# Batch 0's queries in one load, and the last 128 tokens stored in output order by one transfer per column piece, in a linear-attention and SwiGLU kernel

## The chip, the cores and the metric

The kernel runs on one core of a Trainium2 chip. The metric is the device time of that core in microseconds (us), as the median of three executions. The profile is of one execution; its span goes from the first to the last instruction and is a little shorter than the device time.

The core has a matmul engine (PE), a vector engine (DVE), an engine for activation functions (ACT), a general engine (POOL) and a sync engine (SP). Data moves between device memory and on-chip memory by DMA, issued here from SP (queue 1, and ACT for two stores at the end) and from POOL (queue 0, which also casts float32 to bfloat16). PE writes to PSUM, which has eight banks here, each [128 partitions x 512] float32.

## The reference

An attention without a softmax over pairs, then a SwiGLU feed-forward block over all tokens:

```python
# q, k, v: [8 batches, 8 heads, 576 positions, 64], float32
q_s = softmax of q over the 64 features
k_s = softmax of k over the 576 positions
kv  = einsum('bhsd,bhse->bhde', k_s, v)        # a 64x64 matrix for each head
att = einsum('bhsd,bhde->bhse', q_s, kv)
x   = att.transpose(0, 2, 1, 3).reshape(4608, 512)
g   = x @ w_gate                               # [512, 1536]
out = ((g * sigmoid(g)) * (x @ w_val)) @ w_out # [1536, 512]
```

The output is [4608, 512] in float32.

## The kernel before

Tokens of a batch are held in an order of their own. Position s of a batch is s = 9 p + t, with p from 0 to 63 and t from 0 to 8; a partition of the loaded tiles holds nine neighbouring positions of one head. The transposed attention output `xt` has column 64 t + p of a batch. The nine t are handled in two groups, `BANKS = ((0, 5), (5, 9))`, of 320 and 256 tokens. Four heads make a group `G` (two groups, `NG`), and batch 0 is computed by code of its own, in which loads and the first matmuls are laid beside each other.

The loads at the start, the first exponentials and the weight loads (cuts are marked with `# ...`):

```python
kd = []
for G in range(NG):
    load("q", q, 0, G, BANKS[:1] if G == 1 else ((0, T),))
    kd.append(load("k", k, 0, G))
d = nc.gpsimd.dma_start(out=v16[0], in_=head_ap(v, 0, 0))
tc.add_manual_dep(d.ins, kd[0].ins.name, SYNC, reason="order of loads")
for t0, t1 in BANKS:
    nc.gpsimd.dma_start(out=v16[1][:, :, 64 * t0:64 * t1], in_=head_ap(v, 0, 1, t0, t1))
# ...
exp_of("q", 0, 0, BANKS)
exp_of("k", 0, 0)
exp_of("q", 0, 1, BANKS[:1])
first = norm_sum(0, 0, BANKS)
norm_mul(0, 0, BANKS)
norm_sum(0, 1, BANKS[:1])

for c0, n in ((0, 128), (128, 128), (256, 128), (384, 256), (640, 384), (1024, 512)):
    w_slice(wg, moe_w_gate, c0, n)
    w_slice(wv, moe_w_val, c0, n)
    if c0 == 0:
        t0, t1 = BANKS[1]
        nc.gpsimd.dma_start(
            out=raw["q", 0, 1][:, :, 64 * t0:64 * t1], in_=head_ap(q, 0, 1, t0, t1)
        )
w_dma = [wo_slice(m0, 3) for m0 in (0, 3, 6, 9)]
```

`spin` runs matmuls on zeros. `key_sum` and `kv_first` are matmuls over the exponentials of the keys, `scale_first` divides and gives `kn`, `turn_pe` transposes the normalised queries on PE into a PSUM bank, `turn_out` copies them out, `x_mm` forms the attention output and `x_out` copies it to `xt`. A bank of PSUM comes free for its next use when its reader is done. The order at the start of the feed-forward part, with blocks 0 and 1 of the 12 blocks of 128 hidden columns in parts by bank (`i`) and by group (`G`):

```python
spin(8)
spin(6, first)
key_sum(0)
turn_pe(0, 0, 0)
turn_pe(0, 0, 1)
turn_out(0, 0, 0, nc.scalar)
exp_of("k", 0, 1)
turn_out(0, 0, 1, nc.scalar)
norm_mul(0, 1, BANKS[:1])
spin(6)
kv_first(0)
key_sum(1)
scale_first(0, nc.scalar)
turn_pe(0, 1, 0)
turn_out(0, 1, 0, nc.vector)
xp0 = x_mm(0, 0, 0), x_mm(0, 0, 1)
kv_first(1, *BANKS[0])
kv_first(1, *BANKS[1])
# ... scale_first(1), the copies x_out of group 0
x_out(0, 1, 0, x_mm(0, 1, 0))
exp_of("q", 0, 1, BANKS[1:])
norm_sum(0, 1, BANKS[1:])
norm_mul(0, 1, BANKS[1:])
# ...
part_mm(0, 0, 0)
part_mm(0, 0, 1)
sg0 = part_silu(0, 0)
part_mm(1, 0, 0)
turn_pe(0, 1, 1)
turn_out(0, 1, 1, nc.vector)
part_mul(0, 0, sg0)
part_mm(1, 0, 1)
sg1 = part_silu(1, 0)
part_mm(0, 1, 0)
x_out(0, 1, 1, x_mm(0, 1, 1))
part_mul(1, 0, sg1)
part_mm(1, 1, 0)
part_mm(0, 1, 1)
# ... silu and product of the second bank, part_mm(1, 1, 1)

after = w_dma[0]          # batch 1's loads wait for the first slice of w_out
# ... loads of batches 1 to 3 on SP
for m in range(2, MT):
    m_unit(0, S, m)
# ... batch 1's exponentials, output matmuls of the first tokens, its transposes,
# its kv matmuls, and then a loop over chunks of 512 tokens
```

A block of the hidden layer (`m_unit`), the stores and the end of the kernel:

```python
def m_unit(c0, n, m, by_group=False):
    ms = slice(m * 128, (m + 1) * 128)
    parts = [(c0, n)] if n <= 512 else [(c0, 320), (c0 + 320, n - 320)]
    # ... gate (g_ps) and value (u_ps): four matmuls each for each part
    for g_ps, u_ps, (c, w_) in zip(gu[0], gu[1], parts):
        r = c % RING
        sg = ff.tile([128, 512], BF16, tag="sg", name="sg")
        nc.scalar.activation(out=sg[:, 0:w_], in_=g_ps[:, 0:w_], func=AF.Silu)
        nc.vector.tensor_mul(hr[:, m, r:r + w_], sg[:, 0:w_], u_ps[:, 0:w_])

    def store(j, o_sb, c0=0, c1=512, engs=(nc.sync, nc.sync)):
        for half in range(2):
            b, t = divmod(2 * j + half, T)
            dst = bass.AP(
                tensor=out.tensor,
                offset=out[b * S + t, c0].offset,
                ap=[[T * d_model, 64], [1, c1 - c0]],
            )
            engs[half].dma_start(out=dst, in_=o_sb[64 * half:64 * half + 64, c0:c1])

    def o_last(j):
        r0 = (j * 128) % RING
        o_sb = osb.tile([128, 512], FP32, tag="o_sb", name="o_sb")
        for c0, n in ((0, 320), (320, 192)):
            o_ps = bank("o_ps")
            for m in range(MT):
                nc.tensor.matmul(
                    out=o_ps[:, 0:n], lhsT=hr[:, m, r0:r0 + 128], rhs=wo[:, m, c0:c0 + n],
                    start=(m == 0), stop=(m == MT - 1),
                )
            nc.vector.tensor_copy(out=o_sb[:, c0:c0 + n], in_=o_ps[:, 0:n])
            store(j, o_sb, c0, c0 + n, (nc.sync, nc.scalar))
# ...
        o_unit(jo + 3)
        last = n_tok // 128 - 4
        for j in range(last, last + 3):
            o_unit(j)
        o_last(last + 3)
```

A block of 128 output tokens holds two values of t, 64 positions each, so it is stored by two transfers, one from partitions 0 to 63 and one from 64 to 127. The rows of one transfer lie nine rows apart in the output.

Of the kernel before, what the change touches and what calls it, by code (L numbers as in the profile page):

```python
# [15 lines left out]
def kernel(  # L16
# [10 lines left out]
    nc = tc.nc  # L27
# [55 lines left out]
    def load_kv(b):  # L83
        whole = ((0, T),)
        last = b == B - 1
        for G in range(NG):
            load("k", k, b, G, BANKS if last else whole)
            load("v", v, b, G, BANKS if last and G == 0 else whole)

# [26 lines left out]
    def exp_of(what, b, G, pieces=((0, T),)):  # L116
        s = st.setdefault((b, G), {})
        if "e" + what not in s:
            s["e" + what] = at.tile([128, T, 2, 64], BF16, tag="e" + what, name="e" + what)
        e = s["e" + what]  # L120
        src = raw[what, b, G].rearrange("p h (t d) -> p t h d", d=64)
        for t0, t1 in pieces:
            nc.scalar.activation(out=e[:, t0:t1], in_=src[:, t0:t1], func=AF.Exp)  # L123
# [7 lines left out]
    def norm_sum(b, G, pieces=((0, T),)):  # L131
        s = st[b, G]
        eq2 = s["eq"].rearrange("p t h d -> p (t h) d")
        if "rs" not in s:
            s["rs"] = at.tile([128, 2 * T], FP32, tag="rs", name="rs")
            s["rr"] = at.tile([128, 2 * T], FP32, tag="rr", name="rr")
        rs, rr = s["rs"], s["rr"]
# [6 lines left out]
        r = slice(2 * pieces[0][0], 2 * pieces[-1][1])  # L144
        nc.vector.reciprocal(out=rr[:, r], in_=rs[:, r])
        return first

    def norm_mul(b, G, pieces=((0, T),), engs=None):
        s = st[b, G]
        eq2 = s["eq"].rearrange("p t h d -> p (t h) d")  # L150
        if "qs" not in s:
            s["qs"] = at.tile([128, T, 128], BF16, tag="qs", name="qs")
        qs = s["qs"]
# [124 lines left out]

    def m_unit(c0, n, m, by_group=False):
        ms = slice(m * 128, (m + 1) * 128)  # L280
# [14 lines left out]
        for g_ps, u_ps, (c, w_) in zip(gu[0], gu[1], parts):  # L295
            r = c % RING
            sg = ff.tile([128, 512], BF16, tag="sg", name="sg")
            nc.scalar.activation(out=sg[:, 0:w_], in_=g_ps[:, 0:w_], func=AF.Silu)  # L298
            nc.vector.tensor_mul(hr[:, m, r:r + w_], sg[:, 0:w_], u_ps[:, 0:w_])  # L299

    def store(j, o_sb, c0=0, c1=512, engs=(nc.sync, nc.sync)):
        for half in range(2):
            b, t = divmod(2 * j + half, T)
            dst = bass.AP(
                tensor=out.tensor,
                offset=out[b * S + t, c0].offset,
                ap=[[T * d_model, 64], [1, c1 - c0]],
            )
            engs[half].dma_start(out=dst, in_=o_sb[64 * half:64 * half + 64, c0:c1])

# [19 lines left out]
    def o_last(j):  # L330
        r0 = (j * 128) % RING
        o_sb = osb.tile([128, 512], FP32, tag="o_sb", name="o_sb")
        for c0, n in ((0, 320), (320, 192)):
            o_ps = bank("o_ps")
# [5 lines left out]
            nc.vector.tensor_copy(out=o_sb[:, c0:c0 + n], in_=o_ps[:, 0:n])  # L340
            store(j, o_sb, c0, c0 + n, (nc.sync, nc.scalar))

# [3 lines left out]
    with tc.manual_schedule():  # L346
        kd = []
        for G in range(NG):
            load("q", q, 0, G, BANKS[:1] if G == 1 else ((0, T),))
            kd.append(load("k", k, 0, G))  # L350
# [30 lines left out]
        w_dma = [wo_slice(m0, 3) for m0 in (0, 3, 6, 9)]  # L381
# [63 lines left out]
        x_out(0, 0, 1, xp0[1])  # L445
        x_out(0, 1, 0, x_mm(0, 1, 0))
        exp_of("q", 0, 1, BANKS[1:])
        norm_sum(0, 1, BANKS[1:])
        norm_mul(0, 1, BANKS[1:])

        parts = [(64 * t0, 64 * (t1 - t0)) for t0, t1 in BANKS]
        gu = {}

        def part_mm(m, i, G):
            c, w_ = parts[i]
            if G == 0:
                gu[m, i] = bank("g_ps"), bank("u_ps")
            for a in range(2):
                for kk in (2 * G, 2 * G + 1):
                    nc.tensor.matmul(  # L460
                        out=gu[m, i][a][:, 0:w_], lhsT=(wg, wv)[a][:, kk, m * 128:(m + 1) * 128],
                        rhs=xt[:, kk, c:c + w_], start=(kk == 0), stop=(kk == KT - 1),
                    )

        def part_silu(m, i):
            w_ = parts[i][1]
            sg = ff.tile([128, 512], BF16, tag="sg", name="sg")
            nc.scalar.activation(out=sg[:, 0:w_], in_=gu[m, i][0][:, 0:w_], func=AF.Silu)
            return sg

        def part_mul(m, i, sg):
            c, w_ = parts[i]
            nc.vector.tensor_mul(hr[:, m, c:c + w_], sg[:, 0:w_], gu[m, i][1][:, 0:w_])

        part_mm(0, 0, 0)
        part_mm(0, 0, 1)
        sg0 = part_silu(0, 0)
        part_mm(1, 0, 0)
        turn_pe(0, 1, 1)
        turn_out(0, 1, 1, nc.vector)  # L480
        part_mul(0, 0, sg0)
        part_mm(1, 0, 1)
        sg1 = part_silu(1, 0)
        part_mm(0, 1, 0)
        x_out(0, 1, 1, x_mm(0, 1, 1))
        part_mul(1, 0, sg1)
        part_mm(1, 1, 0)
        part_mm(0, 1, 1)
        part_mul(0, 1, part_silu(0, 1))
        part_mm(1, 1, 1)  # L490
        part_mul(1, 1, part_silu(1, 1))

# [12 lines left out]

        for m in range(2, MT):
            m_unit(0, S, m)

# [49 lines left out]
        for ci, (c0, n) in enumerate(chunks):  # L558
# [5 lines left out]
            for m in range(MT):  # L564
# [79 lines left out]
```

## Time and profile before

| what | before |
|---|---|
| time, median of 3 | 314.97 us (314.6 to 315.17) |
| span of the profiled execution | 312.8 us |
| mean granted clock of PE | 0.996 |
| busy: PE, weight loads, DVE, ACT, POOL | 303.6, 150.0, 161.4, 146.2, 32.6 us |
| matmuls | 2182 |
| read from and written to device memory | 37.75 and 9.44 MB |
| end of the last PE instruction | about 307.9 us |

Busy time is a sum over the whole span, and PE's is modelled; so it says which engine is full, and the stretches and waits say when it isn't. A row of the profile names engine, source line, operation, output and inputs; behind an arrow in brackets stands what ended the idle time before it. `xN` means that N such instructions are merged in the row.

### The profile page before, as it was taken

The numbers are of one execution on the slowest core, as the hardware profiler recorded it, in microseconds if no ns is written. First come the engines' busy times: TensorE is split into PE (matmuls) and PEld (weight loads), VectorE is DVE, ScalarE is ACT, GpSimd is POOL, SyncE is SP. The second block draws the span as 40 slices with busy tenths as digits, with TensorE's granted clock in tenths as the row PEclk, the third lists the DMA queues.
The fourth block names the chain that finished last, engine by engine and source line by source line (L and its number), as shares of the span: only waits on it lengthen the run. The fifth ranks groups of instructions, "written<-read, shape, count | busy, mean of one in ns | idle before, by whom it ended". The sixth has DMA issues, their size and how long they took to land.

```text
span 312.8 us, 5455 instructions
## 1 busy us (share of the span) xinstructions
PE 303.6 (97%) x2182; PEld 150.0 (48%) x2182; DVE 161.4 (52%) x275; ACT 146.2 (47%) x214; POOL 32.6 (10%) x40
## 2 busy tenths in 40 slices
PE   6989999999999999999999999999999999999993
PEld 2568754555444544454444444544444444444442
DVE  3664477956763567355826492639353324333321
ACT  5653377794764465547364737455043113212200
POOL 2970011420200110002000200000000000000000
PEclk9999999999999999999999999999999999999998
DMA  7999999999355906491629352605310211021033
GB/s 266 183 191 206 264 390 385 353 181 377 107 105 137 385 14 133 91 385 49 143 67 339 119 116 62 185 0 106 72 34 0 69 25 42 3 67 31 2 80 91
DMA packets 42586, 45.78 MB, mean 146 GB/s; under 512 B 19584, under 2 KB 27520, under 8 KB 42560
## 3 DMA queue, kind: packets, MB, share of 16 engines
q1 hardware_dynamic: 33568, 39.72, 43.5%
q0 software_dynamic: 8832, 5.57, 12.1%
q8 instruction: 17, 0.28, 0.4%
q10 hardware_dynamic: 160, 0.13, 0.2%
q14 instruction: 9, 0.07, 0.1%
HBM read 37.75 MB, written 9.44 MB: 151 GB/s over the span
## 4 chain that ended last, share of the span: by engine, by line
PE 93%; DMA 3%; POOL 2%; ACT 0%; issue 0%; SPq 0%; DVE 0%
PE g_ps L291 30%; PE u_ps L291 29%; PE o_ps L316 29%; DMA wv<-in_moe_w_val_dram 2%; DMA k<-in_k_dram 2%; PE kv L196 2%; PE xp L252 1%; PE o_ps L336 1%; PE u_ps L460 1%; POOL wg L96 0%; POOL v L354 0%; PE tp L171 0%; PE g_ps L460 0%; POOL v L351 0%; POOL wv L96 0%; POOL q L378 0%
## 5 line engine op out<-in xcount | busy, mean ns | idle before, releaser
L298 ACT ACTIVATE sg<-g_ps 128x512 bf16<-128x512 f32 (+2 forms) x116 | 63.2, 559 | 132.7 <-PE g_ps L291 132.3
L299 DVE TENSOR_TENSOR hr<-sg,u_ps 128x512 bf16<-128x512 bf16 (+2 forms) x116 | 72.5, 636 | 85.0 <-PE u_ps L291 81.0
L291 PE MATMUL g_ps<-xt,wg 128*128 128x512 bf16 (+2 forms) x464 | 108.9, 360 | 0.1
L291 PE MATMUL u_ps<-xt,wv 128*128 128x512 bf16 (+2 forms) x464 | 108.9, 360 | 0.0
L316 PE MATMUL o_ps<-wo,hr 128*128 128x512 bf16 x420 | 93.9, 379 | 0.0
L291 PEld LDWEIGHTS <-wv 128*128 128x128 bf16 x464 | 45.4, 98 | 46.0
L291 PEld LDWEIGHTS <-wg 128*128 128x128 bf16 x464 | 44.8, 98 | 44.9 <-issue 0.4
L316 PEld LDWEIGHTS <-hr 128*128 128x128 bf16 x420 | 40.9, 98 | 48.6
L110 DVE COPY o_sb<-o_ps 128x512 f32<-128x512 f32 x33 | 22.4, 680 | 39.2 <-PE o_ps L316 39.2
L126 POOL CAST vb<-v 128x1152 bf16<-128x1152 f32 x14 | 16.9, 1211 | 138.7 <-DMA v<-in_v_dram 102.9
L140 DVE TENSOR_REDUCE rs<-eq 128x18 f32<-128x1152 bf16 (+2 forms) x18 | 21.8, 1214 | 13.2 <-ACT eq L123 13.2
L156 DVE TENSOR_TENSOR qs<-eq,rr 128x1152 bf16<-128x1152 bf16 (+2 forms) x18 | 22.1, 1233 | 0.2
L123 ACT ACTIVATE eq<-q 128x1152 bf16<-128x1152 f32 (+2 forms) x18 | 18.3, 1051 | 2.9 <-DMA q<-in_q_dram 2.8
L123 ACT ACTIVATE ek<-k 128x1152 bf16<-128x1152 f32 (+2 forms) x17 | 17.9, 1102 | 0.2
L298 ACT ACT_TABLE_LOAD x11 | 14.1, 1283 | 0.2
L123 ACT ACT_TABLE_LOAD x11 | 14.1, 1283 | 0.2
L386 PE MATMUL idle<-zero 128*128 128x512 bf16 x20 | 7.8, 555 | 2.9 <-DVE rs L140 1.6
L266 ACT CAST xt<-xp 128x512 bf16<-128x512 f32 x14 | 7.8, 586 | 5.2 <-PE xp L252 5.2
L267 DVE CAST xt<-xp 128x512 bf16<-128x512 f32 x14 | 9.0, 683 | 0.7 <-PE xp L252 0.7
L196 PEld LDWEIGHTS <-ek 64*64 64x64 bf16 x504 | 6.3, 107 | 1.7 <-ACT qt L108 0.4
L196 PE MATMUL kv<-vb,ek 64*64 64x65 bf16 x504 | 6.8, 194 | 0.0
L252 PE MATMUL xp<-qt,kn 64*64 64x512 bf16 (+1 forms) x112 | 6.7, 292 | 0.0
(51 smaller groups left out, 80.0 us busy)
## 6 DMA issues: line engine op xcount, KB each, us to landing
out_dram<-o_sb SPq DMA_DIRECT2D x70, 128.0 KB, 2.3
q<-in_q_dram SPq DMA_DIRECT2D x15, 576.0 KB, 5.3
k<-in_k_dram SPq DMA_DIRECT2D x13, 576.0 KB, 7.9
v<-in_v_dram SPq DMA_DIRECT2D x13, 576.0 KB, 8.9
wo<-in_moe_w_out_dram POOLq DMA_DIRECT2D x4, 384.0 KB, 15.2
k<-in_k_dram SPq DMA_DIRECT2D x3, 320.0 KB, 7.7
k<-in_k_dram SPq DMA_DIRECT2D x3, 256.0 KB, 7.9
wg<-in_moe_w_gate_dram POOLq DMA_DIRECT2D x1, 512.0 KB, 10.6
```

The lines of the kernel that those rows point to most:

```text
L110: eng.tensor_copy(out=out, in_=in_)
L123: nc.scalar.activation(out=e[:, t0:t1], in_=src[:, t0:t1], func=AF.Exp)
L126: return nc.gpsimd.tensor_copy(out=vbs[G][:, :, :, 0:64], in_=raw["v", b, G].rearrange("p h (t d) -> p t h d", d=64),)
L140: i = nc.vector.reduce_sum(out=rs[:, 2 * t0:2 * t1], in_=eq2[:, 2 * t0:2 * t1, :], axis=mybir.AxisListType.X)
L156: last = eng.tensor_mul(qs[:, t0:t1, :].rearrange("p t (h d) -> p (t h) d", d=64), eq2[:, 2 * t0:2 * t1, :], s["rr"][:, 2 * t0:2 * t1].to_ ...
L196: nc.tensor.matmul(out=kv[g][HALF[h], c:c + 65], lhsT=ek[HALF[g], t, h, :], rhs=vbs[G][HALF[g], t, h, :], start=(t == 0), stop=(t == T - 1),)
L252: nc.tensor.matmul(out=o[h][HALF[g], c:c + 64 * (t1 - t0)], lhsT=kn[HALF[h], g, G, :], rhs=qt[G][HALF[h], t0:t1, 64 * g:64 * g + 64], star ...
L267: nc.vector.tensor_copy(out=xt[:, 2 * G + 1, c0:c0 + 512], in_=main[G][1])
L291: nc.tensor.matmul(out=gu[a][i][:, 0:w_], lhsT=(wg, wv)[a][:, kk, ms], rhs=xt[:, kk, c:c + w_], start=(kk == 0), stop=(kk == KT - 1),)
L298: nc.scalar.activation(out=sg[:, 0:w_], in_=g_ps[:, 0:w_], func=AF.Silu)
L299: nc.vector.tensor_mul(hr[:, m, r:r + w_], sg[:, 0:w_], u_ps[:, 0:w_])
L316: nc.tensor.matmul(out=o_ps, lhsT=hr[:, m, r0:r0 + 128], rhs=wo[:, m, :], start=(m == 0), stop=(m == MT - 1),)
```

## The change

At the start, batch 0's second query group is loaded whole, ahead of the second keys; the late load on POOL's queue and the staged order of blocks 0 and 1 are gone, and `m_unit` makes all twelve blocks. At the end, the last 128 tokens are put in pair order when the hidden values are written: column 2 p + h takes the place of 64 h + p. Then partitions 2 p and 2 p + 1 of the last output block hold two neighbouring rows of the output, and one transfer over 64 row pairs stores a column piece, in place of two. The 320-column piece goes by ACT, the 192-column piece by SP. Some loads of batches 6 and 7 are also split in two.

```diff
-            load("k", k, b, G, BANKS if last else whole)
-            load("v", v, b, G, BANKS if last and G == 0 else whole)
+            load("k", k, b, G, BANKS if last or (b == B - 2 and G == 1) else whole)
+            load("v", v, b, G, BANKS if last else whole)
 # ... (m_unit)
-            nc.vector.tensor_mul(hr[:, m, r:r + w_], sg[:, 0:w_], u_ps[:, 0:w_])
+            w1 = w_ - 128 if final else w_
+            nc.vector.tensor_mul(hr[:, m, r:r + w1], sg[:, 0:w1], u_ps[:, 0:w1])
+            if final:
+                nc.vector.tensor_mul(
+                    hr[:, m, r + w1:r + w_].rearrange("k (p h) -> k h p", h=2),
+                    sg[:, w1:w_].rearrange("k (h p) -> k h p", h=2),
+                    u_ps[:, w1:w_].rearrange("k (h p) -> k h p", h=2),
+                )
 # ... (o_last)
-        for c0, n in ((0, 320), (320, 192)):
+        b, t = divmod(2 * j, T)
+        for c0, n, eng in ((0, 320, nc.scalar), (320, 192, nc.sync)):
 # ...
-            store(j, o_sb, c0, c0 + n, (nc.sync, nc.scalar))
+            dst = bass.AP(
+                tensor=out.tensor,
+                offset=out[b * S + t, c0].offset,
+                ap=[[T * d_model, 64], [d_model, 2], [1, n]],
+            )
+            eng.dma_start(out=dst, in_=o_sb[:, c0:c0 + n])
 # ... (the start)
-            load("q", q, 0, G, BANKS[:1] if G == 1 else ((0, T),))
+            load("q", q, 0, G)
 # ...
-        exp_of("q", 0, 1, BANKS[:1])
+        exp_of("q", 0, 1, BANKS)
 # ...
-        norm_sum(0, 1, BANKS[:1])
+        norm_sum(0, 1, BANKS)
 # ...
-            if c0 == 0:
-                t0, t1 = BANKS[1]
-                nc.gpsimd.dma_start(
-                    out=raw["q", 0, 1][:, :, 64 * t0:64 * t1], in_=head_ap(q, 0, 1, t0, t1)
-                )
 # ...
-        norm_mul(0, 1, BANKS[:1])
+        norm_mul(0, 1, BANKS)
 # ...
         turn_pe(0, 1, 0)
+        turn_pe(0, 1, 1)
         turn_out(0, 1, 0, nc.vector)
+        turn_out(0, 1, 1, nc.vector)
 # ...
-        x_out(0, 1, 0, x_mm(0, 1, 0))
 # ... (the late exponential, sum and product; part_mm, part_silu, part_mul and their order: removed)
+        xp1 = x_mm(0, 1, 0), x_mm(0, 1, 1)
+        x_out(0, 1, 0, xp1[0])
+        x_out(0, 1, 1, xp1[1])
 # ...
-        for m in range(2, MT):
-            m_unit(0, S, m)
+        for m in range(MT):
+            m_unit(0, S, m, by_group=(m == 0))
 # ...
-                m_unit(c0, n, m, by_group=(ci == 0 and m == 0))
+                m_unit(c0, n, m, by_group=(ci == 0 and m == 0), final=final)
```

More of the change, by code (lines that the diff above doesn't have):

```diff
@@ L117, in exp_of @@
         s = st.setdefault((b, G), {})
-        if "e" + what not in s:
-            s["e" + what] = at.tile([128, T, 2, 64], BF16, tag="e" + what, name="e" + what)
-        e = s["e" + what]
+        e = s["e" + what] = at.tile([128, T, 2, 64], BF16, tag="e" + what, name="e" + what)
         src = raw[what, b, G].rearrange("p h (t d) -> p t h d", d=64)
@@ L133, in norm_sum @@
         eq2 = s["eq"].rearrange("p t h d -> p (t h) d")
[L134 to L137, printed above, removed]
+        rs = at.tile([128, 2 * T], FP32, tag="rs", name="rs")
         first = None
@@ L143, in norm_sum @@
             first = first or i
-        r = slice(2 * pieces[0][0], 2 * pieces[-1][1])
-        nc.vector.reciprocal(out=rr[:, r], in_=rs[:, r])
+        rr = s["rr"] = at.tile([128, 2 * T], FP32, tag="rr", name="rr")
+        nc.vector.reciprocal(out=rr, in_=rs)
         return first
@@ L150, in norm_mul @@
         eq2 = s["eq"].rearrange("p t h d -> p (t h) d")
-        if "qs" not in s:
-            s["qs"] = at.tile([128, T, 128], BF16, tag="qs", name="qs")
-        qs = s["qs"]
+        qs = s["qs"] = at.tile([128, T, 128], BF16, tag="qs", name="qs")
         for (t0, t1), eng in zip(pieces, engs or (nc.vector, nc.vector)):
@@ L275, in x_and_next_kv, with m_unit @@
             scale_both(b + 1)
-    def m_unit(c0, n, m, by_group=False):
+    def m_unit(c0, n, m, by_group=False, final=False):
         ms = slice(m * 128, (m + 1) * 128)
@@ L298, in m_unit, with store @@
             nc.scalar.activation(out=sg[:, 0:w_], in_=g_ps[:, 0:w_], func=AF.Silu)
-            nc.vector.tensor_mul(hr[:, m, r:r + w_], sg[:, 0:w_], u_ps[:, 0:w_])
-    def store(j, o_sb, c0=0, c1=512, engs=(nc.sync, nc.sync)):
+            w1 = w_ - 128 if final else w_
[6 more added lines that the diff above has]
+                )
+    def store(j, o_sb):
         for half in range(2):
@@ L305, in store @@
                 tensor=out.tensor,
-                offset=out[b * S + t, c0].offset,
-                ap=[[T * d_model, 64], [1, c1 - c0]],
+                offset=out[b * S + t, 0].offset,
+                ap=[[T * d_model, 64], [1, d_model]],
             )
-            engs[half].dma_start(out=dst, in_=o_sb[64 * half:64 * half + 64, c0:c1])
+            nc.sync.dma_start(out=dst, in_=o_sb[64 * half:64 * half + 64, :])
     def o_mm(j, o_ps=None, m0=0, m1=MT):
@@ L445 @@
         x_out(0, 0, 1, xp0[1])
-        x_out(0, 1, 0, x_mm(0, 1, 0))
[L447 to L491, printed above, removed]
+        xp1 = x_mm(0, 1, 0), x_mm(0, 1, 1)
+        x_out(0, 1, 0, xp1[0])
+        x_out(0, 1, 1, xp1[1])
         after = w_dma[0]
```

## The prediction

> **What bounds the kernel now.** I read the chain that ended last first, then busy time by stretch, then the two ends in order of time, because a nearly full engine leaves only the ends to gain. Part 4 of the page (shares of the span by engine):
>
> ```profile
> PE 93%; DMA 3%; POOL 2%; ACT 0%; issue 0%; SPq 0%; DVE 0%
> ```
>
> The matmul engine (PE) carries 93%. Busy time by stretch (start:end, length, then PE, weight loads, DVE, ACT, POOL in us with counts, granted clock, DMA share, GB/s):
>
> ```profile
> 20.00:100.00 80.00, 79.92 (x696) 45.34 (x695) 48.53 (x87) 49.47 (x76) 11.49 (x10) 1.00 0.92 248
> 100.00:200.00 100.00, 100.00 (x791) 46.77 (x790) 56.55 (x90) 55.61 (x72) 6.91 (x6) 1.00 0.57 165
> 200.00:295.00 95.00, 95.00 (x454) 43.02 (x455) 41.28 (x64) 29.10 (x47) 0.00 (x0) 1.00 0.18 40
> ```
>
> From 20 us to 295 us PE idles 0.08 us in all, at full clock. The change leaves the useful matmuls as they are in number and width, so the time can move in two places: how early PE becomes full, and how long the end lasts after its last matmul. The start, in order of time (start, duration, engine, line, what, idle before):
>
> ```profile
> 14.09 0.45 PE L460 MATMUL g_ps<-xt,wg 128*128 128x320 bf16 x2
> ...
> 16.34 0.11 PEld L460 LDWEIGHTS <-wg 128*128 128x128 bf16 x2 [1.15 <-DMA wg<-in_moe_w_gate_dram]
> ...
> 16.89 0.11 PEld L460 LDWEIGHTS <-wv 128*128 128x128 bf16 x2 [0.43 <-DMA wv<-in_moe_w_val_dram]
> ...
> 20.15 1.14 PE L291 MATMUL g_ps<-xt,wg 128*128 128x320 bf16 x8
> ```
>
> The first feed-forward matmul starts at 14.09, and the third block (m=2) at 20.15. Between them lie blocks 0 and 1. A block of 576 tokens takes 1.96 us (the chain has 0.98 for the gate's eight matmuls and 0.98 for the value's), so 3.92 us; the second bank's transposes take 0.26 and its output matmuls 0.23. The other 1.6 us are waits, 1.15 and 0.43 of them for the second slices of the two weights.
>
> [...]the 128 KB stores land 2.3 us after issue. [...]stores from 64 partitions move at most 219 GB/s near the end while one queue stores (263 in one short slice where two queues run), loads into 128 partitions 389 GB/s at 4 to 6 us. [...]The trace has such a product at 0.48 us for 320 columns and 0.69 for 512: 1.1 ns a column and about 0.13 fixed.
>
> **The change at the start.** It removes the late load of the last 256 columns of batch 0's second query group, and the interleaving of blocks 0 and 1 with it; the queries now come whole ahead of the second keys. It adds 256 KB to the first queue and takes 256 KB, with one POOL issue of 0.76 us, from the weight queue.
>
> First, what comes later. Landing times before, from issue plus time to landing: first queries 4.7, first keys 6.15, 320 query columns 7.1, second keys 8.5, first values 10.45, second values 11.9 and 12.6, first weight slices 13.3 and 14.2, late queries 14.8, second weight slices 16.3 and 16.85. The loads go at about 390 GB/s, so 256 KB cost 0.65 us: queries 7.7, keys 9.15, second values about 12.5 and 13.2, first weights about 14 and 14.8. The keys' exponential starts only at 10.57, behind ACT's copy of the first transposes, so the keys have room. DVE gains one reduction (0.69) and one product (0.69) ahead of the transposes, which have room before 12.2. PE gets four more transposes (0.27) before its first output matmuls, and kn of the second group comes about 0.3 us later, at 14.1 for 13.8. Then four matmuls, a wait for DVE's 0.42 us copy that frees their bank, four more (0.23): the first feed-forward matmul at about 14.85, 0.75 later than now.
>
> Second, what comes back. From 14.85 the blocks run without a gap. Block 0 ends at 16.8; the weights of block 1 are there (16.3, perhaps 0.4 sooner with one POOL issue less; its value weights, 16.85, are needed at 17.8). Block 2 starts at 18.8 (its weights land at 17.6 and 18.3). That is 20.15 - 18.8 = 1.35 us earlier. I checked the later slices in the same way: the tightest value slice lands at 24.85 and would be wanted at 25.6.
>
> Third, what of it lasts. Batch 1's keys are a gate that does not move with PE: their loads are held until the first output weights have landed (31.84)[...]. Rows of ACT and PE, and the time to landing of the load issued at 33.79:
>
> ```profile
> 46.86 2.31 ACT L123 ACTIVATE ek<-k 128x1152 bf16<-128x1152 f32 x3
> ...
> 50.04 0.80 PE L196 MATMUL kv<-vb,ek 64*64 64x65 bf16 x72
> ```
> ```profile
> k<-in_k_dram SPq DMA_DIRECT2D x1, 576.0 KB, 12.4
> ```
>
> The keys land at 33.79 + 12.4 = 46.2, and ACT uses them at about 46.9, so only 0.7 us of a lead fits in front; after these exponentials comes the copy that lets kv start at 50.04. Whole query rows and one POOL issue less may bring the loads forward by 0 to 0.3. I keep 0.8 of the 1.35 us. PE loses the rest as new idle between 44 and 50 us. After that PE is full and the lead stays.
>
> **The change at the end.** The last m blocks split the product: 384 columns and 128 in pair order, 0.55 + 0.27 = 0.82 us for 0.69 by the fit above, twelve times 0.13 = 1.6 us of DVE. In that chunk DVE idles 1.04 us of each 1.73, and the last token block is used over 9 us after the last product (295.7 to 305.1), so none of it is on the path. The tail before, in order of time, and then the times to landing of its stores:
>
> ```profile
> 305.33 0.69 DVE L110 COPY o_sb<-o_ps 128x512 f32<-128x512 f32 x1 [1.90 <-PE o_ps L316]
> 306.96 0.49 DVE L340 COPY o_sb<-o_ps 128x320 f32<-128x320 f32 x1 [0.94 <-PE o_ps L336]
> 307.48 1.39 ACTq L309 DMA_DIRECT2D out_dram<-o_sb  x2
> 307.95 0.36 DVE L340 COPY o_sb<-o_ps 128x192 f32<-128x192 f32 x1 [0.50 <-PE o_ps L336]
> ```
> ```profile
> out_dram<-o_sb SPq DMA_DIRECT2D x1, 80.0 KB, 2.0
> out_dram<-o_sb ACTq DMA_DIRECT2D x1, 80.0 KB, 2.4
> out_dram<-o_sb ACTq DMA_DIRECT2D x1, 48.0 KB, 3.1
> out_dram<-o_sb SPq DMA_DIRECT2D x1, 48.0 KB, 2.9
> ```
>
> The last copy ends at 308.31 and the last pair is issued at about 308.35; they land at 311.3 and 311.4, and 1.4 us of closing follow. The smallest transfers are the slowest[...]. After the change one transfer of 96 KB takes the place of the pair, with the same row pieces (768 bytes) and bytes.[...] I take 0.4 us off.
>
> Sum: 0.8 + 0.4 = 1.2 us; 314.97 - 1.2 = 313.8 us (the median time stands 2.2 us above the profiled span of 312.8, which I take as fixed). The split of batch 6's and 7's loads only moves which earlier transfer an issue must see finished; PE has no wait there (95.00 of 95.00), so it gets nothing.
>
> **Rivals.** (a) The start gets worse: the staged loads were put there to give PE work at 14.09, and if the second values or first weights slip by more than my 0.65 us, PE starts at 16 or later and the lead at 20 us turns negative: +0.5 to +1 us, total about 315.2. For it: weight loads were the wait that ended last here. Against it: the same bytes stand ahead of the second weight slices in both. (b) All of the lead holds, because the load gate also moves or PE finds other work: start -1.4, total 313.2. For it: PE has output matmuls as filler around 44 to 50.[...] (c) [...]a single transfer gains nothing, or its one queue makes it slower than two: 0 to +0.2, total 314.2. For it: two halves already ran beside each other on two queues. (d) The split product delays the last blocks: +0.3 at most, and DVE's 1.04 us idle speaks against it.
>
> **Range and chances.** The start lies between -1.4 and +0.5, the tail between -0.75 and +0.2. Both ends together are unlikely, so eight times in ten between 312.9 and 315.1. Two per cent is 6.3 us, more than either end holds apart from a load order gone wrong: faster 0.01, same 0.97, slower 0.02.
>
> **What would show it.** Block 2 starts at about 18.8, with no waits for second weight slices; the first feed-forward matmul at about 14.9; PE loses some 0.5 us between 44 and 50; the kv matmuls of batch 1 start near 49.2 rather than 50.04; from the last copy's end to the end of the span 4.1 us rather than 4.5, with the last store landing 2.2 to 2.6 us after issue. I am wrong if the first feed-forward matmul comes after 15.8, if block 2 is not ahead of 20.15, or if the 96 KB store takes 2.9 us or more.

## The result, and the profile after

| | before | after |
|---|---|---|
| time, median of 6 executions each | 315.06 us (314.56 to 316.05) | 311.38 us (311.09 to 311.75) |
| ratio of the times, 95% interval | | 0.9883 (0.9865 to 0.9900) |
| span of the profiled execution | 312.8 us | 309.7 us |
| end of the last copy out of PSUM | 308.31 us | 306.36 us |
| from there to the end of the span | 4.49 us | 3.34 us |
| PE busy from 14 to 20 us | 5.08 us | 6.00 us |

The change makes the kernel 3.7 us faster (1.2%), three times what I predicted, and below my range of 312.9 to 315.1. In the two profiles the start gives 308.31 - 306.36 = 1.95 us and the end 4.49 - 3.34 = 1.15 us; over all profiles the end is worth nearer 0.5 us, as shown below.

The shares of the chain that ended last, part 4 of the page after, and then busy time by stretch, in the columns of before:

```profile
PE 96%; DMA 1%; DVE 0%; ACT 0%; issue 0%
```
```profile
20.00:100.00 80.00, 79.89 (x729) 44.76 (x730) 48.52 (x86) 49.50 (x74) 12.30 (x10) 1.00 0.91 255
100.00:200.00 100.00, 100.00 (x754) 46.63 (x747) 57.28 (x95) 55.70 (x73) 6.91 (x6) 1.00 0.55 161
200.00:295.00 95.00, 95.00 (x455) 43.00 (x454) 41.27 (x70) 28.11 (x44) 0.00 (x0) 1.00 0.17 37
```

PE was full in the middle before and is so now. The 3% that DMA had in the chain before are now 1%: the value weights, in it from 11.7 to 16.9 us before, have left it. The start after, PE alone, in order of time:

```profile
13.84 0.45 PE L202 MATMUL xp<-qt,kn 64*64 64x320 bf16 x8 [0.42 <-DVE kn L424]
14.22 0.66 PE L284 MATMUL g_ps<-xt,wg 128*128 128x320 bf16 x4
...
16.20 1.14 PE L284 MATMUL g_ps<-xt,wg 128*128 128x320 bf16 x8
...
18.16 1.14 PE L284 MATMUL g_ps<-xt,wg 128*128 128x320 bf16 x8
```

Blocks 0, 1 and 2 start at 14.22, 16.20 and 18.16, just under 2 us apart, and no row has a wait for weights. Before, block 2 came at 20.15, so it gains 1.99 us. From its start to the end of the last copy it is 288.16 us before and 288.20 us now: the gain of the start arrives at the end almost whole. The second slices landed at 15.2 (gate) and 15.95 (value), from their issue times plus times to landing; they are wanted at 16.1 and 17.1.

Batch 1's keys after, ACT and PE in order of time, and the landing of the load issued at 33.77:

```profile
45.21 2.31 ACT L121 ACTIVATE ek<-k 128x1152 bf16<-128x1152 f32 x3 [0.24 <-DMA k<-in_k_dram]
...
48.12 0.80 PE L189 MATMUL kv<-vb,ek 64*64 64x65 bf16 x72
```
```profile
k<-in_k_dram SPq DMA_DIRECT2D x1, 576.0 KB, 11.4
```

The keys land at 33.77 + 11.4 = 45.2, one microsecond sooner than before, and ACT waits for them for 0.24 us. The kv matmuls start at 48.12 for 50.04, 1.92 us sooner, so nearly the whole lead has come through. The tail after, in order of time, and the times to landing of its last stores:

```profile
305.02 0.49 DVE L342 COPY o_sb<-o_ps 128x320 f32<-128x320 f32 x1 [0.94 <-PE o_ps L338]
305.54 0.66 ACTq L348 DMA_DIRECT2D out_dram<-o_sb  x1
306.00 0.36 DVE L342 COPY o_sb<-o_ps 128x192 f32<-128x192 f32 x1 [0.50 <-PE o_ps L338]
306.39 0.61 SPq L348 DMA_DIRECT2D out_dram<-o_sb  x1
```
```profile
out_dram<-o_sb ACTq DMA_DIRECT2D x1, 160.0 KB, 2.3
out_dram<-o_sb SPq DMA_DIRECT2D x1, 96.0 KB, 2.1
```

The last store lands 2.1 us after its issue, for 2.9 and 3.1 of the pair before, although it is twice as large as each of them; 1.2 us of closing follow (the waits with which the program ends).

### The profile page after: what moved, and what is told of

It is laid out like the page before. It is cut to its first block, busy times and chain, and to the rows that moved or that the text cites. A ratio compares the mean times of both kernels' runs of the same rounds, so it can differ in the third digit from the quotient of the medians.

```text
span 309.7 us, 5467 instructions
## 1 busy us (share of the span) xinstructions
PE 302.8 (98%) x2182; PEld 150.3 (49%) x2182; DVE 161.9 (52%) x286; ACT 146.3 (47%) x214; POOL 32.8 (11%) x39
## 4 chain that ended last, share of the span: by engine, by line
PE 96%; DMA 1%; DVE 0%; ACT 0%; issue 0%
PE g_ps L284 30%; PE u_ps L284 30%; PE o_ps L317 29%; PE kv L189 2%; PE xp L245 1%; PE idle L388 1%; DMA q<-in_q_dram 1%; PE tp L164 1%; PE o_ps L338 1%; DVE rs L135 0%; PE xp L202 0%; PE kv L411 0%; ACT eq L121 0%; ACT xt L259 0%; PE ks L397 0%; DVE o_sb L342 0%
## 5 line engine op out<-in xcount | busy, mean ns | idle before, releaser
L291 ACT ACTIVATE sg<-g_ps 128x512 bf16<-128x512 f32 (+2 forms) x120 | 64.7, 554 | 133.6 <-PE g_ps L284 120.5
L293 DVE TENSOR_TENSOR hr<-sg,u_ps 128x512 bf16<-128x512 bf16 (+3 forms) x120 | 72.5, 616 | 86.3 <-PE u_ps L284 80.7
L284 PE MATMUL g_ps<-xt,wg 128*128 128x512 bf16 (+2 forms) x480 | 111.4, 358 | 0.1
L284 PE MATMUL u_ps<-xt,wv 128*128 128x512 bf16 (+2 forms) x480 | 111.3, 358 | 0.0
L284 PEld LDWEIGHTS <-wv 128*128 128x128 bf16 x480 | 46.9, 98 | 46.4
L284 PEld LDWEIGHTS <-wg 128*128 128x128 bf16 x480 | 46.3, 98 | 45.5 <-issue 0.6
L124 POOL CAST vb<-v 128x1152 bf16<-128x1152 f32 x14 | 17.8, 1277 | 135.8 <-DMA v<-in_v_dram 106.6
```

The lines of the kernel that those rows point to most:

```text
L124: return nc.gpsimd.tensor_copy(out=vbs[G][:, :, :, 0:64], in_=raw["v", b, G].rearrange("p h (t d) -> p t h d", d=64),)
L284: nc.tensor.matmul(out=gu[a][i][:, 0:w_], lhsT=(wg, wv)[a][:, kk, ms], rhs=xt[:, kk, c:c + w_], start=(kk == 0), stop=(kk == KT - 1),)
L293: nc.vector.tensor_mul(hr[:, m, r:r + w1], sg[:, 0:w1], u_ps[:, 0:w1])
```

## The experiments

### One half of the change at a time

The first kernel has the new start with the old end. Its edit against the changed kernel:

```diff
 # (m_unit: the product in one piece, old token order)
-            w1 = w_ - 128 if final else w_
-            nc.vector.tensor_mul(hr[:, m, r:r + w1], sg[:, 0:w1], u_ps[:, 0:w1])
-            # ... the product in pair order
+            nc.vector.tensor_mul(hr[:, m, r:r + w_], sg[:, 0:w_], u_ps[:, 0:w_])
 # (o_last)
-            eng.dma_start(out=dst, in_=o_sb[:, c0:c0 + n])      # one transfer, 64 row pairs
+            store(j, o_sb, c0, c0 + n, (nc.sync, nc.scalar))    # two transfers, 64 rows each
```

> The new start and the new load splits, with the end of before (two stores for each column piece, tokens in their old order). Theory (two independent gains: 1.95 us from the start, 1.15 us from the end, both read from the spans of before and after, 312.8 and 309.7): PE is without a gap from 14.2 us on, the last copy ends near 306.4, and 4.4 to 4.6 us follow it as in before; time about 312.7 for 315.06 of before and 311.38 of the change. Rival (the two ends are not independent[...]): the last copy ends elsewhere than 306.2 to 306.6, or the tail is not 4.5 us.

Measured: 312.31 us (ten executions, ratio to before 0.9903, interval 0.9876 to 0.9929). The last copy ends at 306.18 and 3.92 us follow. So most of the gain, 314.99 - 312.31 = 2.7 us, is in the start. The tail was shorter than the 4.4 to 4.6 expected, and the time lower than 312.7: the tail of 4.49 in the one profile of before was long for this form of end.

The second kernel has the old start and load splits with the new end, the opposite edit, made in the kernel before.

> The start and the load splits of before, with the new end alone (pair order, one store for each column piece). Theory: last copy ends near 308.3 as in before, then 3.3 us instead of 4.5; time about 313.9. My prediction's size of the tail gain (0.4 us) would give 314.7. Rival (the split product delays the last blocks): the last copy ends later than 308.5.

Measured: 315.26 us, ratio to before 0.9995 (0.9969 to 1.0021), which looks like no gain. But its 20 executions are two groups of ten: 313.59 to 314.50 us with mean granted clocks of 0.997 to 1.0, and 316.02 to 316.60 with 0.989 to 0.995. The kernel before, on the same chip, has the same two groups: 28 executions with clocks over 0.995, median 314.66, and 17 with 0.995 or less, median 317.05. Within the upper clocks the new end gives 314.66 - 313.82 = 0.84 us. In its profile 3.53 us follow the last copy. The last copy ended at 309.07, later than 308.5, which the rival had as its mark; but block 2 began at 20.94 in this execution, 0.79 us later than in the profile of before, and the last copy came 0.76 us later. So the lateness arose at the start and not at the split product. The two groups have experiments of their own, below.

### Which part of the start

The old start and old end, with the second query group loaded whole:

```diff
-            load("q", q, 0, G, BANKS[:1] if G == 1 else ((0, T),))
+            load("q", q, 0, G)
 # ...
-            if c0 == 0:
-                t0, t1 = BANKS[1]
-                nc.gpsimd.dma_start(
-                    out=raw["q", 0, 1][:, :, 64 * t0:64 * t1], in_=head_ap(q, 0, 1, t0, t1)
-                )
```

> Before with one edit: the second query group is loaded whole ahead of the second keys, and the late load of 256 columns is gone from POOL's queue; the staged order of blocks 0 and 1 is kept, and so is the old end. Theory A (the late load is what cost the time: it stood in front of the second weight slices and held them back): the waits of 1.15 and 0.43 us for the second weight slices shrink to under 0.3 in all, block 2 starts at 18.2 to 18.6 for 20.15, time about 313.3. Theory B (the staged order itself costs, with transposes and output matmuls between parts): block 2 stays after 19.3 and the time above 314.3.

Measured: 314.13 us (ratio 0.9954, 0.9935 to 0.9973). Theory A failed. Theory B has the place of block 2 right, but the time lies 0.2 us under its mark. PE in this kernel, in order of time:

```profile
15.21 0.43 PE L455 MATMUL g_ps<-xt,wg 128*128 128x320 bf16 x2
16.72 0.45 PE L455 MATMUL u_ps<-xt,wv 128*128 128x320 bf16 x2 [1.08 <-DMA wv<-in_moe_w_val_dram]
...
19.94 1.14 PE L291 MATMUL g_ps<-xt,wg 128*128 128x320 bf16 x8
```

The gate slice of block 1 does come in time now: its matmuls start at 15.21 without a wait, for 16.35 before. But the staged order asks for the value slice right afterwards, and that lands at 16.7, much as before. Block 2 starts at 19.94. So the load alone is worth about 0.9 us in the median, and the plain order the other 1.8 us (314.13 to 312.31). A part of the 0.9 is rarer drops of the clock (below): 2 of these 20 executions have a mean clock of 0.995 or less, for 17 of 45 before, and among the others the gain is 314.66 - 314.08 = 0.6 us. The plain order gives PE the whole of block 0, 1.96 us, before it asks for block 1's weights; the staged order has only the first bank of block 0, four runs of 0.27 us, because in the program the rest of block 0 stands behind the first parts of block 1. It asks for the two slices about 1 us and 1.7 us sooner. It also puts the second bank's transposes and output matmuls, about 0.5 us, among the blocks, where the plain order has them ahead of block 0; what this adds was not measured by itself.

### Is the landing of batch 1's keys a gate?

My prediction let 0.55 of 1.35 us be lost to it. First, the loads of batch 1 held back longer:

```diff
-        after = w_dma[0]
+        after = w_dma[1]
```

> The changed kernel with one edit: batch 1's loads wait for the second instead of the first slice of the output weights, which comes 1.5 to 2 us later. Theory of my prediction (batch 1's keys are a gate: their landing at 45.2 in the changed kernel is just when they are wanted, 45.0): keys land near 46 to 47, kv of batch 1 starts 1 to 1.8 us later than 48.12, PE gets gaps of that size between 44 and 50, and the time rises by about as much, to 312.4 to 313.2. Rival (there is slack left behind the keys, or the landing follows bytes and not the gate): kv starts within 0.4 of 48.12 and the time stays within 0.4 of the changed kernel's 311.4.

Measured: 311.55 us, and 309.7 us of span as in the changed kernel. The keys' load is issued at 35.30 rather than 33.77 and lands after 10.1 us, at 45.4; kv starts at 48.08. So 1.5 us of delay in the issue did not move the landing. This kernel doesn't yet say what a later landing would cost. For that, one load of batch 2's queries went ahead of the keys:

```diff
         for what, src in (("q", q), ("v", v), ("k", k)):
+            if what == "k":
+                load("q", q, 2, 0)
             for G in range(NG):
 # ... (and the same load taken out of batch 2's)
```

> The changed kernel with one load of batch 2's queries moved ahead of batch 1's keys, so that the keys land later, by about 1.4 us for 576 KB. In the changed kernel the keys land at 45.2, ACT waits 0.24 us for them, and kv of batch 1 starts 2.9 us after the landing. Theory of my prediction (keys landing at 46.2 or later take back part of the lead): keys land at 46.4 to 46.9, kv starts 2.9 us later, at 49.3 to 49.8 rather than 48.1, and the time rises by 1.0 to 1.7 us to 312.4 to 313.1. Rival (PE has other work to fill in): kv may be later but the time stays under 311.8.

Measured: 312.46 us (312.21 to 312.81). ACT and PE in order of time:

```profile
46.87 2.31 ACT L121 ACTIVATE ek<-k 128x1152 bf16<-128x1152 f32 x3 [1.71 <-DMA k<-in_k_dram]
...
48.24 0.82 PE L189 MATMUL kv<-vb,ek 64*64 64x65 bf16 x56
...
49.24 0.32 PE L189 MATMUL kv<-vb,ek 64*64 64x65 bf16 x16 [0.17 <-ACT ek L121]
```

The keys land at 46.9 and ACT waits 1.71 us. PE starts kv on time and then stops in it for the last keys; its last copy ends at 306.99 for 306.36, and 0.2 us of that were lost earlier, at a first block starting at 14.42. From block 2 to the last copy it is 288.64 us for 288.20. So the gate is there, but 1.7 us of lateness cost about 0.4 us in the trace and 0.6 to 1.1 in the time (changed kernel: 311.38 and, on another chip, 311.85; on the same chip, without the load splits, 311.77). The expected 1.0 to 1.7 was too much. The gate can cost something without the added load too: in the repetition of the changed kernel below the keys landed at 45.6, PE waited 0.28 us for ACT's exponential of them at 46.84, and block 2 to the last copy took 288.46 us.

### The end: the count of transfers or the order of the rows?

First the pair order kept, and two transfers again for each column piece:

```diff
-            dst = bass.AP(..., ap=[[T * d_model, 64], [d_model, 2], [1, n]])
-            eng.dma_start(out=dst, in_=o_sb[:, c0:c0 + n])
+            for half, eng in ((0, nc.sync), (1, nc.scalar)):
+                dst = bass.AP(..., offset=out[b * S + 32 * half * T + t, c0].offset,
+                              ap=[[T * d_model, 32], [d_model, 2], [1, n]])
+                eng.dma_start(out=dst, in_=o_sb[64 * half:64 * half + 64, c0:c0 + n])
```

> The changed kernel with its pair order kept, but each column piece stored by two transfers again (32 row pairs each, from partitions 0-63 by SP and 64-127 by ACT). It separates the count of transfers from the order of the rows. Theory 1 (what helps is one issue in place of two[...]): the time goes back by most of the 0.8 to 0.9 us that the two runs with one half of the change give for the end, to 312.1 to 312.4, as with the old end on the new start (312.3). Theory 2 (the neighbouring rows are what helps): it stays at 311.4 to 311.6.

Measured: 312.11 us (311.97 to 312.74), 3.90 us after the last copy, as with the old end on the new start (3.92). Neighbouring rows give nothing by themselves. The times to landing of its last pair, SP's own waits at its end, and then those of the changed kernel (line, what it waited for: us in all, times, longest):

```profile
out_dram<-o_sb SPq DMA_DIRECT2D x1, 48.0 KB, 2.3
out_dram<-o_sb ACTq DMA_DIRECT2D x1, 48.0 KB, 2.0
```
```profile
SPq L600 <- DMA out_dram<-o_sb: 1.4, 2, 1.2
```
```profile
SPq L600 <- DMA out_dram<-o_sb: 0.9, 2, 0.6
```

The last pair lands 2.3 and 2.0 us after issue here, close to the single transfer's 2.1. What differs is mostly SP's wait for stores in the closing, 1.4 for 0.9 us. In all profiles with pairs this wait is 1.4 to 2.1 us, and with single transfers over 64 row pairs 0.6 to 0.9. Why it is longer with pairs is not shown: the landing alone does not set it, since the last pair of the staged order with the whole load landed after 2.8 and 2.6 us with 3.83 us from the last copy to the end, and that of the new start with the old end after 1.9 and 2.2 us with 3.92.

Then the old token order with one transfer, written as 2 times 64 rows, and no split product:

```diff
-                ap=[[T * d_model, 64], [d_model, 2], [1, n]],
+                ap=[[d_model, 2], [T * d_model, 64], [1, n]],
```

> The changed kernel with the last 128 tokens in their old order (no split product), and still one transfer for each column piece, written as 2 times 64 rows. It asks whether the pair order is needed for the single transfer. Theory 1[...]: the last transfer runs on 2 engines and lands 5 us or more after its issue, the time rises by 3 us or more, to 314.5 or above. Theory 2 (the order doesn't matter to the transfer): lands 2.1 us after issue as in the changed kernel, time 311.3 to 311.5.

Measured: 316.87 us, 8.4 us after the last copy. Busy time by stretch at its end (the last two columns are the DMA share and GB/s):

```profile
308.00:309.00 1.00, 0.00 (x0) 0.00 (x0) 0.00 (x0) 0.00 (x0) 0.00 (x0) 0.63 0.13 35
...
311.00:312.00 1.00, 0.00 (x0) 0.00 (x0) 0.00 (x0) 0.00 (x0) 0.00 (x0) 0.50 0.13 45
```

A DMA share of 0.13 is, as an estimate, the time of 2 of 16 engines (0.13 x 16 = 2.1), at 31 to 50 GB/s from 307 to 313. In the changed kernel, with 64 times 2 rows, the last two stores move at a share of 0.64 and 214 GB/s from 307 to 308, and have landed at 308.5. Why the share is so low with 2 times 64 rows the runs don't show. So the pair order is not for neighbouring rows; with it one transfer can be written as 64 times 2 rows, and that form is what was fast here.

### The two groups of executions

Two more profiled executions of the kernel with the old start and the new end:

> A second look at the kernel with the old start and the new end, half of whose executions take 316.0 to 316.6 us. If this one is of that group, theory: the profile shows the granted clock at 0.5 for about 3.4 us between 16 and 24 us, as in the kernel with exchanged slices[...]. If it is of the other group: clock 1.0 throughout.

> A third look at the kernel with the old start and the new end, with the same expectations as the second: an execution near 316 us has the clock at 0.5 for about 3.4 us after the waits for weights, one near 314 us has it at 1.0 throughout.

The first took 313.84 us, with clock 1.0 throughout and waits of 1.43 and 0.51 us for the second slices. The second took 318.47. Its start, weight loads and PE in order of time, and then busy time by stretch:

```profile
17.75 0.11 PEld L474 LDWEIGHTS <-wg 128*128 128x128 bf16 x2 [2.67 <-DMA wg<-in_moe_w_gate_dram]
17.75 0.45 PE L474 MATMUL g_ps<-xt,wg 128*128 128x320 bf16 x2 [2.34 <-DMA wg<-in_moe_w_gate_dram]
...
18.53 0.13 PEld L474 LDWEIGHTS <-wv 128*128 128x128 bf16 x2 [0.67 <-DMA wv<-in_moe_w_val_dram]
18.53 0.72 PE L474 MATMUL u_ps<-xt,wv 128*128 128x320 bf16 x2 [0.33 <-DMA wv<-in_moe_w_val_dram]
```
```profile
16.00:18.00 2.00, 0.25 (x2) 0.11 (x2) 0.14 (x1) 0.78 (x2) 0.82 (x2) 1.00 1.65 185
18.00:20.00 2.00, 1.34 (x9) 0.57 (x8) 1.45 (x3) 1.57 (x2) 2.00 (x4) 0.56 1.44 188
20.00:22.00 2.00, 2.00 (x10) 1.04 (x8) 0.82 (x2) 0.44 (x1) 1.64 (x3) 0.50 1.33 203
22.00:24.00 2.00, 2.00 (x13) 1.32 (x13) 0.82 (x2) 0.48 (x2) 1.09 (x2) 0.50 1.30 202
24.00:26.00 2.00, 2.00 (x15) 1.49 (x14) 0.84 (x2) 0.66 (x2) 0.00 (x0) 0.74 1.26 208
```

The gate slice came 1.4 us later than in the first execution. PE was busy for 0.25 us between 16 and 18, and then the granted clock (third column from the right) is 0.56, 0.50, 0.50 and 0.74: a little under 7 us at half speed, in which a pair of 320-column matmuls takes 0.72 for 0.45 us. Here PE's weight loads waited 2.67 us just before the clock fell and 0.67 us as it did; with waits of 1.43 and 0.51 us, in the first execution, it stayed at 1.0.

Two kernels test whether the waits bring the drop, both with the old start and the new end. In the first, the second and third weight slices change places, so PE waits longer:

```diff
-        for c0, n in ((0, 128), (128, 128), (256, 128), (384, 256), (640, 384), (1024, 512)):
+        for c0, n in ((0, 128), (256, 128), (128, 128), (384, 256), (640, 384), (1024, 512)):
```

> The kernel with the old start and the new end, with the second and third weight slices exchanged in the load order, so that block 1's weights come 1.3 to 1.5 us later and PE waits longer for them, about 3 us in all. Theory[...]: the profile shows a granted clock well under 1.0 in the stretch of 16 to 22 us, all executions have mean clocks of 0.995 or less, and the time is 317 to 318.5: 313.9, plus 1.4 of waiting, plus 1.5 to 2.5 for the clock. Rival (no drop): clock 1.0 in all stretches, time 315.0 to 315.6.

Measured: 316.70 us; 17 of 20 executions have clocks of 0.995 or less. In its profile PE's weight load waits 3.50 us, and the clock is 0.96, 0.50 and 0.68 in the stretches from 16, 18 and 20 us, some 3.4 us at half speed. Three executions kept a clock of 1.0 and took 314.8 to 315.0; the median of the other 17 is 316.77. So with the longer wait the drop was usual, not certain (17 of 20 executions, for ten of 20 without the exchange), and within this kernel the drop costs about 1.9 us, of which 3.4 us at half speed account for 1.7. In the second, matmuls on zeros fill the wait:

```diff
         sg0 = part_silu(0, 0)
+        spin(6)
         part_mm(1, 0, 0)
```

> The kernel with the old start and the new end, with six matmuls on zeros put into PE's wait for the second weight slices. That kernel's executions fall into two groups: 313.6 to 314.5 us with a mean granted clock of 0.997 to 1.0, and 316.0 to 316.6 with 0.989 to 0.995. Theory (the waits for weights at 15 to 17 us leave PE idle enough that its clock is halved for some 3 us in about half of the executions): with the wait filled, the second group vanishes, nearly all executions lie at 313.6 to 314.8 with clocks of 0.996 or more, median near 314.0 for 315.3. Rival (the second group has another cause, such as the loads): about half of the executions stay above 316.

Measured: 314.46 us for 315.26; three of 20 executions have clocks of 0.995 or less, for ten of 20. The second group shrank, as theory has it, but did not vanish, and one execution took 317.0 us at clock 1.0; that one stays unexplained.

Over all comparisons the kernel before had a clock of 0.995 or less in 43 of 118 executions, the changed kernel in none of 12. Over all kernels with the new start, without the one of the 2 times 64 rows, it is 2 of 56; one of these two, at 314.64 us, stands 2.3 us above its kernel's median. So drops became rare and did not vanish. The mean clock is only a rough sign of a drop at 16 to 24 us, since it is taken over the whole span. The idle end is in it: all 20 executions with the store of 2 times 64 rows have 0.994 or less, and in that profile the clock is 1.00 from 12 to 300 us and falls after 308. So is the time ahead of the first block: in the profile of the kernel with the late keys, at a mean of 0.995, PE waited 2.00 us up to 6.64, for the first sums of the queries, and a little later ran at half clock for over 3 us (0.50 from 8 to 10 us and 0.71 from 10 to 12):

```profile
8.00:10.00 2.00, 2.00 (x21) 1.42 (x20) 1.70 (x4) 1.53 (x3) 2.00 (x4) 0.50 1.06 218
```

Of the 43 executions of before, 37 also took more than 316 us; the other six took 315.05 to 315.70.

### The load splits, a repetition on one chip, and what comes next

The changed kernel without the new splits:

```diff
-            load("k", k, b, G, BANKS if last or (b == B - 2 and G == 1) else whole)
-            load("v", v, b, G, BANKS if last else whole)
+            load("k", k, b, G, BANKS if last else whole)
+            load("v", v, b, G, BANKS if last and G == 0 else whole)
```

> The changed kernel without the new splits of batch 6's and 7's loads. Theory (they only shift which earlier transfer an issue must see finished, and PE has no wait there): 311.2 to 311.7, PE full from 100 to 295 us. Rival (the new number of transfers at the end needs the splits, or the last stores wait for older ones): the time rises by 0.3 us or more and the last stores are issued later than 0.1 us after their copies.

Measured: 311.77 us on one chip, 0.4 over the changed kernel on another, with PE full from 100 to 295 us and the last store issued on time. The runs below, all on one chip, set that right.

> The changed kernel again, for comparison on one chip with the three others of this group. Expected 311.1 to 311.8, with mean granted clocks of 0.996 or more in all executions.

> The changed kernel without the new splits of batch 6's and 7's loads, beside the changed kernel on the same chip. If the splits do nothing for the time: within 0.2 us of the changed kernel. If the 0.4 us seen before between two chips was theirs: 0.3 to 0.5 above it.

> The new start with the old end, beside the changed kernel on the same chip: the whole worth of the new end in one difference. From the earlier runs 0.7 to 1.0 us above the changed kernel; if my prediction's size (0.4) were right, 0.3 to 0.5.

Measured, six executions each: the changed kernel 311.85 (311.42 to 312.63), without splits 311.96 (311.61 to 313.38), the old end on the new start 312.12 (311.63 to 312.64). The splits do nothing that these times show. The new end's 0.27 us is inside the scatter of either. The profiles measure it better, because they take out the start: from the last copy to the end of the span twelve profiles with single transfers over 64 row pairs have 3.13 to 3.55 us, and the five with two transfers 3.83, 3.84, 3.90, 3.92 and 4.49. The end is thus worth about 0.5 us; 1.15 in the first pair of profiles was an unusual tail before.

Last, three warm-up matmuls in place of six ahead of the first kv matmuls:

```diff
         norm_mul(0, 1, BANKS)
-        spin(6)
+        spin(3)
```

> The changed kernel with three matmuls on zeros in place of six ahead of the first kv matmuls. In the changed kernel these six stand in the chain that ended last, 1.35 us from 10.17. Theory A (they hold back what follows): the first feed-forward matmul comes 0.3 to 0.6 us earlier and the time falls to 310.8 to 311.1. Theory B (the second values, landing at 13.0, and the first value weights, at 14.5, are next in line): at most 0.2 us earlier, 311.2 to 311.6.

Measured: 311.53 us (311.34 to 312.37), within the scatter of the changed kernel. The first feed-forward matmul came at 14.17 in its profile, and then the second gate slice, which landed at 16.9 in this execution for 15.2, was waited for, 0.86 us. The loads come next, as theory B has it; this is no clear gain.

## Why the prediction was wrong

**Where the time is.** Right. Only the two ends moved, PE stayed full between them, and neither the split product nor the splits of loads show: from block 2 to the last copy it is 288.13 to 288.31 us in 14 of the 16 profiles without a clock drop in the blocks, of both starts and both ends. The other two are the late keys (288.64) and the repetition of the changed kernel (288.46).

**What comes later at the start.** The landing times were near (second values 13.0, first weights 13.7 and 14.5, for 13.2, 14 and 14.8), but the sum "first feed-forward matmul at about 14.85" was 0.6 us too high: it came at 14.22 in the profile after, and at 13.7 to 14.6 in the other profiles of the new start. Two of its terms were not there. The four more transposes did not delay kn: before, the output matmuls of the first group, at first held for kn by 0.17 us, stretched from 12.48 to 13.12; now they run in one piece from 12.70 to 13.14, and the second group's kn is ready at 13.80 for 13.77. And the wait for a bank did not come: the eight output matmuls of the second group run together, 0.45 us.

**What comes back.** Right in mechanism, and by the mis-sized start too small: block 2 at 18.16 rather than 18.8, so 1.99 us for 1.35. The staged order is what cost, as the run with the whole load showed: it asks for the second slices early, and it has some 0.5 us of other matmuls among the blocks. The size was too small because the first term, the first feed-forward matmul, was put too late.

**What of it lasts.** This is the step that failed: "I keep 0.8 of the 1.35 us". The gate is real, as the run with later keys showed, but both numbers in it were wrong. I took 46.2 for the landing from the one profile of before and let it move by at most 0.3; with the new start and the loads in this order it was 45.0 to 45.6 in eight of ten profiles, 45.9 and 46.1 in the other two. Two more profiles with the old start and the old load order have 45.75 and 46.25. So a part of the difference is scatter between executions. And I charged PE in full for what ACT waits, while a wait of 1.7 us cost PE about 0.4. In place of 0.8 of 1.35 us, 1.95 of 1.99 us came through to the last copy. Whether the change itself makes the loads land sooner, from a first issue at the same time (31.82 for 31.84), stays open.

**The end.** Right in direction, and 0.4 us against about 0.5, but the near size is luck: the 0.4 was my estimate, and nothing in the trace of before showed when a single transfer would land. It landed a little sooner than I had it, after 2.1 us for 2.2 to 2.6. But with the pair order kept, a pair lands within 0.2 us of it, and SP's closing wait is 0.5 us longer. What sets that wait stays open. The last stores, issued by SP and ACT, took 1.9 to 3.1 us to land wherever the profiles show it.

**What was not in the sum at all.** The clock. The profile of before has a clock of 1.00 up to 310 us (its mean of 0.996 comes from the idle end), and I took the median of 314.97 as the time of that execution, which itself took 314.60. About a third of the executions of before lie above 316 us at a lower clock. That this is the drop at 16 to 24 us seen with the same start and the new end is likely; no profile of before itself shows it. The groups' medians are 2.4 us apart, and with exchanged slices the drop by itself cost 1.9; the rest would be the longer wait ahead of it. In executions at full clock the change gives 314.7 - 311.4 = 3.3 us or less (2.9 with 311.85); the drops lift before's median by another 0.3 to 0.4. The parts, 1.95 for the start, 0.5 for the end and 0.3 for the drops, make 2.75 of the 3.2 us measured on one chip (315.05 - 311.85) and of the 3.7 of the first comparison; the remainder is not explained.

**The rivals.** (b), that the whole lead holds, was nearest, and still short with 313.2. (a) was wrong in sign. (c), that a single transfer gains nothing, was wrong, though by half a microsecond only. (d) did not show: with and without the split product block 2 to the last copy takes the same time.

## What to carry to other kernels

When work is staged to start sooner on part of the data, ask what the early part will want next and when that lands: here the early start ran out of work after 1.1 us and waited for the very weights that the plain order doesn't need for another microsecond. A lead in front of a load need not be lost by the whole delay that one profile suggests (I kept 0.8 of 1.35 us, and 1.95 of 1.99 came through); take the landing from several profiles, and count only what the matmul engine itself would wait. To store interleaved rows by one transfer, measure how its dimensions are nested: as 64 times 2 rows the transfer here landed in 2.1 us, as 2 times 64 it ran at a DMA share of 0.13 and the kernel ended 8.4 us after the last copy. The order in which the data is written cost nothing that shows: block 2 to the last copy took 288.20 us with the split product and 288.16 without.

## What the runs showed of the hardware that I had not expected

- A wait of PE can cost more than its length: with one of 2.67 us for weights and one of 0.67 close behind it the granted clock fell to 0.5 for nearly 7 us, and after one of 2.00 us early in another kernel for over 3 us. With waits of 1.43 and 0.51 us it stayed at 1.0. One kernel had two times, 313.8 and 316.3 us in ten executions each.
- A single transfer of 2 times 64 rows of 768 bytes ran at a DMA share of 0.13, by my estimate the time of 2 of 16 engines, with 8.4 us from the last copy to the end; as 64 times 2 rows it landed in 2.1 us.
- The second weight slices landed anywhere from 15.0 to 17.7 us (gate) in the profiles of these kernels, from issue times of 10.1 to 11.0 us, and at 16.3, 16.3 and 17.7 in three profiles of one kernel. A start that wants them at 15.2 feels all of that; one that wants them at 16.1 waited for the gate slice in 2 of 11 profiles (0.48 and 0.86 us).
- Holding batch 1's loads back by 1.5 us left the landing of its keys unchanged (45.4 for 45.2 us); one more load ahead of them moved it to 46.9.
